# Attention scores as four 64x64-tiled float32 products, in a fused windowed-attention and feed-forward kernel

## The chip, the cores and the metric

The kernel runs on one core of a Trainium2 chip. The metric is the device time of one execution in microseconds; lower is better. Of the kernel before, three timed runs gave 1008.7 us in the median (1007.8 to 1010.62). The engines of the core are named as in the profile: PE (matmuls; PEld is the same engine loading weights), DVE (vector operations), ACT (activations and casts), POOL, and SP, which issues the DMAs.

## What is computed

Attention over a window of 64 positions for 8 batches of 8 heads, 576 positions, head size 64, all float32; then a feed-forward layer with softplus, 512 to 2048 to 512, for all 4608 tokens.

```python
scores = (1 / np.sqrt(64)) * np.matmul(q, k.transpose(0, 1, 3, 2))
rel = pos[:, None] - pos[None, :]
scores = np.where((rel >= 0) & (rel < 64), scores, -1e9)
attn = np.exp(scores - scores.max(-1, keepdims=True))
attn = attn / (attn.sum(-1, keepdims=True) + 1e-9)
x = np.matmul(attn, v)                      # then to 4608 x 512
h = x @ w_in                                # 512 x 2048
g = np.maximum(h, 0.0) + np.log1p(np.exp(-np.abs(h)))
out = g @ w_out                             # 2048 x 512
```

## The kernel before

The 4608 tokens are cut into 12 blocks of 384 (`TB`), a block into three pieces j of 128 queries (`NJ`). Two heads make a pair `hp`; four pairs make the 512 columns of x. A **task** is one block and one pair: 48 tasks. `attention(g, hp)` is a generator; each `yield` ends a stage. The first two blocks (`by_pe`, 8 tasks) run while the weights are still being loaded and converted, and turn the probabilities on PE (L303) and multiply them with v in float32 (L352). The other 40 tasks split q, k, v and the probabilities into high and low parts, use faster matmuls, and turn the probabilities by DMA.

Because a query sees itself and the 63 positions before it, 128 queries need 192 keys. In the 40 later tasks q is cast and its low part subtracted (L241 on ACT, L242 on DVE), then k (L247, L248). For each j four matmuls of 192 columns (two heads, high and low k) go to one PSUM bank (L267). DVE adds the mask, scales and takes the minimum for each head (L274: an instruction and one that reads its accumulator). Since 192 columns hold 128 for each query half, a fold then lays the outer 64 columns over the first (L280). ACT takes exponentials and sums (L284), DVE normalises (L295). The eight early tasks keep k in `kbd`, two heads on a block diagonal with zeros, and do one float32 product of 384 columns for each j (L263).

`ps_a` has three PSUM banks, taken in turn. Up matmuls (`ffn_up`, L390: 12 of 384 columns into `ps_h`) and down matmuls (`ffn_down`, L411: 9 of 512 columns) are the feed-forward layer: 192 steps, each with one up and one down. ACT takes three functions of the up result (L394 to L396), DVE one (L398), ACT or DVE casts (L400) and DVE subtracts (L401).

What sets the order: each stage, each up and each down has a due time, in halves of a step (up of step n at 2n + 0.5, down at 2n + 5.5). All events are sorted by it. `STG` lists the due times of the stages of a task relative to its base; the bases of later tasks are 8 apart (`SHP`), so a task's attention-times-v (L364, one stage for each head) falls where the scores of the task two further on begin. PE keeps this order as it is written; the instructions of the other engines are ordered by a scheduler at build time. [...]

Of the kernel before, what the change touches and what calls it, by code (L numbers as in the profile page):

```python
# [9 lines left out]
F32 = mybir.dt.float32  # L10
# [7 lines left out]
P = 128  # L18
# [13 lines left out]
STG = (-13, -5.9, -5, 0, 1, 2, 3, 4, 5, 6, 7, 7.1, 12, 14, 16, 17)  # L32
# [11 lines left out]
def window_attention_softplus_ffn(  # L44
# [70 lines left out]
    W = CH + P  # L115

    kbd_s = [att.tile([P, 2, CH + TB], F32, name="kbd", tag=f"k{i}") for i in range(2)]
    for t in kbd_s:  # L120
        nc.vector.memset(t[D:P, 0, :], 0.0)
        nc.vector.memset(t[0:D, 1, :], 0.0)
        nc.vector.memset(t[0:D, 0, 0:CH], 0.0)
        nc.vector.memset(t[D:P, 1, 0:CH], 0.0)

    v3z = cpool.tile([P, 2, NJ, 2, 2, D], BF16, name="v3z")
    v_ts = [att.tile([P, 2, NJ, P], F32, name="v_t", tag=n) for n in ("nat", "tr")]
    for t in v_ts:
        nc.vector.memset(t[0:CH, 0, 0, :], 0.0)
# [4 lines left out]
    mask = cpool.tile([P, W], BF16, name="mask")  # L134
    nc.gpsimd.memset(mask, 0.0)
    nc.gpsimd.affine_select(
        out=mask, in_=mask, pattern=[[1, W]], compare_op=ALU.is_gt, fill=FAR, base=0, channel_multiplier=-1
    )
    nc.gpsimd.affine_select(
        out=mask, in_=mask, pattern=[[-1, W]], compare_op=ALU.is_ge, fill=FAR, base=CH, channel_multiplier=1  # L140
    )

    mask_c = cpool.tile([P, W], BF16, name="mask_c")
    nc.gpsimd.tensor_copy(mask_c, mask)
    nc.gpsimd.memset(mask_c[:, 0:CH], FAR)
    ident = att.tile([P, P], F32, name="ident", tag="xf")
# [9 lines left out]
    def load_w(f):  # L156


        if f < NE + 4:
            k = FIRST[f % 4] if f < NE else (4, 6)[f % 2]  # L160
            parts = [(spare(k, [P, 2, DM], w_words.dtype, "raws"), spare(k + 1, [P, 2, DM], F32, "ws"), 0, 2)]
        else:
            parts = [
                (
                    ff.tile([P, 1, DM], w_words.dtype, name="raw"),
                    att.tile([P, 1, DM], F32, name="wh", tag=("v_in", "v12")[m]),
                    m, m + 1,
                )
                for m in range(2)
            ]  # L170
# [18 lines left out]
    def attention(g, hp):  # L189
# [12 lines left out]
        heads = [slice(0, D), slice(D, P)]  # L202

        if by_pe:
            qf = ld.tile([P, 2, TB], F32, name="q_in") if hp % 2 else ld.tile([P, 2, W - P + TB], F32, name="k_in")
            qf = qf[:, 0, 0:TB]
            kf = kbd_s[hp % 2]
            skip = CH if t0 == 0 else 0
            nc.sync.dma_start(qf, qT[c0 : c0 + P, t0 : t0 + TB])
            for hh in range(2):  # L210
                nc.sync.dma_start(kf[heads[hh], hh, skip:], kT[c0 + hh * D : c0 + (hh + 1) * D, t0 - CH + skip : t0 + TB])
        else:
            q_in = ld.tile([P, 2, TB], F32, name="q_in")
            k_in = ld.tile([P, 2, W - P + TB], F32, name="k_in")
            ts, ks = slice(t0, t0 + TB), slice(t0 - CH, t0 + TB)
            for half in heads:
                nc.sync.dma_start(
                    q_in[half, :, :], qT[c0 : c0 + P, ts].rearrange("(h d) t -> d h t", h=2)
                )
                nc.sync.dma_start(  # L220
                    k_in[half, :, :], kT[c0 : c0 + P, ks].rearrange("(h d) t -> d h t", h=2)
                )
        yield

        if by_pe:
# [12 lines left out]
        else:
            q_hl = att.tile([P, 2, TB], F32R, name="q_hl")
            low = heads[1]  # L240
            nc.scalar.copy(q_hl, q_in)  # L241
            nc.vector.tensor_tensor(  # L242
                q_hl[low, :, :], q_in[low, :, :], q_hl[low, :, :].bitcast(F32), ALU.subtract
            )
            yield
            k_hi, k_lo = [att.tile([P, 2, W - P + TB], F32R, name=f"k{i}") for i in range(2)]
            nc.scalar.copy(k_hi, k_in)  # L247
            nc.vector.tensor_tensor(k_lo, k_in, k_hi.bitcast(F32), ALU.subtract)  # L248
        yield

        if g == 0:

            st = spare(FIRST[hp], [P, 2, NJ, W], F32, "st0")
        else:
            st = att.tile([P, 2, NJ, W], F32, name="st", bufs=2)
        mn = att.tile([P, 2, NJ], F32, name="mn", bufs=2)
        sm = att.tile([P, 2 * NJ], F32, name="sm", bufs=2)
        for j in range(NJ):
            sp = bank()
            spv = sp[:, : 2 * W].rearrange("p (h c) -> p h c", h=2)  # L260
            js, kc = slice(j * P, (j + 1) * P), slice(j * P, j * P + W)
            if by_pe:
                mm(spv, qf[:, js], kf[:, :, kc], start=True, stop=True)  # L263
            else:
                for hh in range(2):
                    for i, part in enumerate((k_hi, k_lo)):
                        mm(  # L267
                            spv[:, hh, :], q_hl[:, hh, js], part[:, hh, kc],
                            start=(hh == 0 and i == 0), stop=(hh == 1 and i == 1), skip_group_check=True,
                        )  # L270
            t = ORDER[g] * NJ + j
            m = mask_c if (t * P) % S == 0 else mask_b if (t * P) % S + P > S else mask
            for hh in range(2):
                nc.vector.tensor_tensor_reduce(  # L274
                    st[:, hh, j, :], spv[:, hh, :], m, QSCALE, 3.0e38, ALU.add, ALU.min, mn[:, hh, j : j + 1]
                )
            yield

        sv = st.rearrange("p h j c -> p (h j) c")
        nc.vector.tensor_tensor(sv[:, :, 0:CH], sv[:, :, 0:CH], sv[:, :, P:], ALU.min)  # L280
        for hh in range(2):
            for j in range(NJ):
                i = hh * NJ + j
                nc.scalar.activation(  # L284
                    sv[:, i, 0:P], sv[:, i, 0:P], AF.Exp, bias=mn[:, hh, j : j + 1], scale=-1.0, accum_out=sm[:, i : i + 1]
                )
# [7 lines left out]
        pn = sv[:, :, 0:P]  # L294
        nc.vector.tensor_tensor(pn, pn, sm.unsqueeze(2).to_broadcast([P, 2 * NJ, P]), ALU.mult)  # L295
        if by_pe:

            yield
            pt = att.tile([P, 2, TB], F32, name="pt", tag="q_hl")
            for hh in range(2):  # L300
                pp = bank()
                for j in range(NJ):
                    tp(pp[:, j * P : (j + 1) * P], sv[:, hh * NJ + j, 0:P], ident)  # L303
                nc.scalar.copy(pt[:, hh, :], pp[:, :TB])
        else:
# [8 lines left out]
            nc.scalar.copy(nat[:, 0, :, :], pn)  # L314
            turn(0)
            yield
            nc.vector.tensor_tensor(nat[:, 1, :, :], pn, nat[:, 0, :, :], ALU.subtract)
            turn(1)
            yield
            v_in = att.tile([P, 2, NJ, P], F32, name="v_in")  # L320

            before, own = [v[t : t + TB, c0 : c0 + P].rearrange("(j p) n -> p j n", p=P) for t in (t0 - CH, t0)]
            nc.sync.dma_start(v_in[:, 0, :, :], before)
            nc.sync.dma_start(v_in[0:CH, 1, :, :], own[CH:P, :, :])
            nc.sync.dma_start(v_in[CH:P, 1, :, :], own[0:CH, :, :])
            yield

            v12 = att.tile([P, 2, NJ, 2, 2, D], BF16, name="v12")
            vv = v_in.rearrange("p u j (h d) -> p (u j h) d", h=2)
            v1, v2, v3 = [t.rearrange("p u j h i d -> p (u j h) i d")[:, :, i, :] for t, i in ((v12, 0), (v12, 1), (v3z, 0))]  # L330
# [15 lines left out]
        else:  # L346
            xf = att.tile([P, TB], F32, name="xf")
        for hh in range(2):
            if by_pe:
                for a in range(2 * NJ):  # L350
                    cs = slice(a * CH, (a + 1) * CH)
                    mm(  # L352
                        av[heads[hh], cs], v_t[:, a % 2, a // 2, heads[hh]], pt[:, hh, cs],
                        start=(a == 0), stop=(a == 2 * NJ - 1), skip_group_check=True,
                    )
                if hh == 1:
                    nc.scalar.copy(x_t[0], av[:, :TB])
# [154 lines left out]
```

## Time and profile before

| | |
|---|---|
| median of the three runs | 1008.7 us |
| the profiled execution, and its span | 1013.1 us, 1011.3 us |
| DMA queue of the kernel | 137152 packets, 99.65 MB, 36.8% of 16 engines' span |
| HBM | 73.66 MB read, 10.22 MB written |

The span is the time from the first to the last instruction; 1.8 us lie around it. In the table of groups each row gives the line, engine, operation, output and inputs, shape and count, then the busy time, the mean duration of one in ns, and the idle time just before them with what ended it. Rows of a timeline begin with a start and a length in us, from the span's start, and merge like instructions that follow each other (`x12`). Matmuls are pipelined: a record lasts longer than the distance to the next one's start, so prices of PE are read from starts. Rows of windows give for each stretch its length, then the busy time and count of PE, PEld, DVE, ACT and POOL, the granted PE clock, the DMA share and GB/s.

### The profile page before, as it was taken

Reading aid. Unit: us, or ns where it says so; the run is one execution under the profiler, and the core shown is the slowest. Engines: PE = TensorE matmul, PEld = TensorE weight load, DVE = VectorE, ACT = ScalarE, POOL = GpSimd, SP = SyncE. Lnnn points to the kernel's source line nnn. Section 1 sums busy time; section 2 is a strip of 40 time slices with the busy share of each in tenths; the row PEclk is TensorE's granted clock in tenths of the full one; section 3 lists DMA queues with packets and bytes.
Section 4 is the critical chain, followed back from the end, with each engine's and each line's share of the span. In section 5 each row is a group of like instructions: output and inputs, shape, how many; then the busy total and the mean of one; then the engine's idle time right before and its main releaser. Section 6 shows DMA issues by size and latency. Waiting matters only on the chain.

```text
span 1011.3 us, 17290 instructions
## 1 busy us (share of the span) xinstructions
PE 959.9 (95%) x6240; PEld 851.7 (84%) x6240; DVE 730.4 (72%) x1689; ACT 710.4 (70%) x1673; POOL 3.7 (0%) x14
## 2 busy tenths in 40 slices
PE   6546999999999999999999999999999999999998
PEld 3335888898988998899899998899889989998997
DVE  6897588787777777787777777777768867864332
ACT  4566678787777777777777677777767767865443
POOL 1000000000000000000000000000000000000000
PEclk9767999999999999999999999999999999999999
DMA  5845234443333434333334344433423423410000
GB/s 171 292 164 174 90 125 115 128 116 102 92 99 82 110 86 98 101 91 103 97 83 113 99 82 99 112 74 91 129 70 90 134 66 82 112 32 17 32 1 32
DMA packets 137238, 100.76 MB, mean 100 GB/s; under 512 B 70080, under 2 KB 129216, under 8 KB 135616
## 3 DMA queue, kind: packets, MB, share of 16 engines
q1 hardware_dynamic: 137152, 99.65, 36.8%
q8 instruction: 49, 0.80, 0.3%
q14 instruction: 37, 0.30, 0.1%
HBM read 73.66 MB, written 10.22 MB: 83 GB/s over the span
## 4 chain that ended last, share of the span: by engine, by line
PE 85%; DMA 6%; DVE 4%; ACT 4%; issue 1%; SPq 0%; ACTq 0%; DVEq 0%
PE ps_h L390 37%; PE ps_o L411 36%; PE ps_a L267 5%; PE ps_a L364 4%; DMA raws<-in_w_words_dram 3%; DMA raw<-in_w_words_dram 2%; ACT st L284 1%; DVE ws L178 1%; PE ps_a L263 1%; ACT ws L176 1%; PE ps_a L352 1%; DVE w L183 0%; DVE st L295 0%; DMA k_in<-in_kT_dram 0%; DVE ws L179 0%
## 5 line engine op out<-in xcount | busy, mean ns | idle before, releaser
L390 PE MATMUL ps_h<-x,w 128*128 128x384 f32 x2304 | 440.0, 339 | 0.6 <-ACT x L373 0.4
L411 PE MATMUL ps_o<-w,g 128*128 128x512 f32 x1728 | 433.9, 395 | 4.3 <-DVE g L401 3.1
L390 PEld LDWEIGHTS ps_h<-x,w 128*128 128x128 f32 x2304 | 404.7, 189 | 11.9 <-DVE u L398 1.0
L411 PEld LDWEIGHTS ps_o<-w,g 128*128 128x128 f32 x1728 | 319.5, 189 | 65.5 <-DVE g L401 5.2
L394 ACT ACTIVATE u<-ps_h 128x384 f32<-128x384 f32 x192 | 94.3, 491 | 198.3 <-PE ps_h L390 191.6
L398 DVE SCALAR_TENSOR_TENSOR u<-ps_h,u 128x384 f32<-128x384 f32 x192 | 106.9, 557 | 112.0 <-ACT u L396 109.3
L401 DVE TENSOR_TENSOR g<-u,g 128x384 fp32r<-128x384 f32 x192 | 106.3, 554 | 27.2 <-ACT g L400 25.9
L284 ACT ACTIVATE st<-st,mn 128x128 f32<-128x128 f32 x288 | 111.4, 388 | 9.4 <-DVE st L280 9.3
L274 DVE CUSTOM_DVE_ANT_0 st<-ps_a,mask 128x192 f32<-128x192 f32 x216 | 68.5, 351 | 50.5 <-PE ps_a L267 49.6
L395 ACT ACTIVATE u<-u 128x384 f32<-128x384 f32 x192 | 100.8, 525 | 4.4
L396 ACT ACTIVATE u<-u 128x384 f32<-128x384 f32 x192 | 100.2, 522 | 4.2
L400 ACT CAST g<-u 128x384 fp32r<-128x384 f32 x112 | 57.3, 512 | 31.9 <-DVE u L398 31.5
L267 PE MATMUL ps_a<-k,q_hl 128*128 128x192 f32 x480 | 76.6, 282 | 0.0
L267 PEld LDWEIGHTS ps_a<-k,q_hl 128*128 128x128 f32 x480 | 66.5, 191 | 3.2
L364 PEld LDWEIGHTS <-v 128*128 128x128 bf16 x960 | 44.1, 98 | 17.3 <-issue 17.3
L284 ACT ACTIVATION_READ_ACCUMULATOR st<-st,mn 128x1 f32 x288 | 53.8, 187 | 0.0
L364 PE MATMUL ps_a<-tr,v 128*128 128x64 f16 x960 | 53.6, 194 | 0.0
L364 PE MATMUL ps_a<-tr,v3z 128*128 128x64 f16 x480 | 50.4, 193 | 0.0
L295 DVE TENSOR_TENSOR st<-st,sm 128x768 f32<-128x768 f32 x48 | 45.9, 957 | 1.5
L371 DVE SCALAR_TENSOR_TENSOR xf<-ps_a,xf 64x384 f32<-64x384 f32 x80 | 43.8, 547 | 3.3 <-ACT xf L370 2.0
L248 DVE TENSOR_TENSOR k<-k_in,k 128x896 fp32r<-128x896 f32 x40 | 43.4, 1084 | 0.0
L364 PEld LDWEIGHTS <-v3z 128*128 128x128 bf16 x480 | 42.8, 98 | 0.0
(77 smaller groups left out, 762.2 us busy)
## 6 DMA issues: line engine op xcount, KB each, us to landing
k_in<-in_kT_dram SPq DMA_DIRECT2D x80, 224.0 KB, 3.6
q_in<-in_qT_dram SPq DMA_DIRECT2D x84, 192.0 KB, 3.9
raws<-in_w_words_dram SPq DMA_DIRECT2D x12, 1024.0 KB, 6.2
v_in<-in_v_dram SPq DMA_DIRECT2D x40, 192.0 KB, 2.6
v_in<-in_v_dram SPq DMA_DIRECT2D x80, 96.0 KB, 2.6
out_dram<-raw SPq DMA_DIRECT2D x12, 512.0 KB, 2.8
raw<-in_w_words_dram SPq DMA_DIRECT2D x8, 512.0 KB, 3.7
out_dram<-raw SPq DMA_DIRECT2D x12, 256.0 KB, 3.0
```

The lines of the kernel that those rows point to most:

```text
L267: mm(spv[:, hh, :], q_hl[:, hh, js], part[:, hh, kc], start=(hh == 0 and i == 0), stop=(hh == 1 and i == 1), skip_group_check=True,)
L274: nc.vector.tensor_tensor_reduce(st[:, hh, j, :], spv[:, hh, :], m, QSCALE, 3.0e38, ALU.add, ALU.min, mn[:, hh, j : j + 1])
L284: nc.scalar.activation(sv[:, i, 0:P], sv[:, i, 0:P], AF.Exp, bias=mn[:, hh, j : j + 1], scale=-1.0, accum_out=sm[:, i : i + 1])
L364: mm(av[:, j * P + u * CH : j * P + (u + 1) * CH], w[:, u, j, hh, :, :], tr[:, s, hh * NJ + j, u * CH : (u + 1) * CH], start=(n == 0), sto ...
L390: mm(hv, weight(0, a, f)[:, c * P : (c + 1) * P], x[b][c], start=(i_mm == 0), stop=(i_mm == 3 * NC - 1))
L394: nc.scalar.activation(u, hv, AF.Abs)
L395: nc.scalar.activation(u, u, AF.Exp, scale=-1.0)
L396: nc.scalar.activation(u, u, AF.Ln, bias=1.0)
L398: nc.vector.scalar_tensor_tensor(gf, hv, 0.0, u, ALU.max, ALU.add)
L400: (nc.scalar.copy if g < 2 or f % 2 else nc.vector.tensor_copy)(gt[0], gf)
L401: nc.vector.tensor_tensor(gt[1], gf, gt[0].bitcast(F32), ALU.subtract)
L411: mm(ops[g][j], gt[a][:, js], weight(1, b, f), start=(first and i == 0), stop=(last and i == 2),)
```

## The change

All blocks compute their scores in float32 without a split. For each half u of 128 queries there are 64 queries and exactly 128 keys. A product has 64 rows to contract (one head), 64 queries and 128 keys; with two heads (rows) and two query halves (columns) four products use the four 64x64 tiles of the array. Each head has one bank for all three j. The split of q and k and the fold go; the mask is 128 wide; q, k and v of all blocks are loaded in one way, with two buffers each and earlier for v; the scores of a later task are one stage instead of three; the early tasks' products with v alternate between the heads. `kbd` and the double layouts of v go, and the tiles for weights converted late share other buffers.

```diff
-STG = (-13, -5.9, -5, 0, 1, 2, 3, 4, 5, 6, 7, 7.1, 12, 14, 16, 17)
+STG = (-13, -5, 0, 3, 4, 5, 6, 7, 12, 14, 16, 17)
...
-            q_hl = att.tile([P, 2, TB], F32R, name="q_hl")
-            low = heads[1]
-            nc.scalar.copy(q_hl, q_in)
-            nc.vector.tensor_tensor(
-                q_hl[low, :, :], q_in[low, :, :], q_hl[low, :, :].bitcast(F32), ALU.subtract
-            )
-            yield
-            k_hi, k_lo = [att.tile([P, 2, W - P + TB], F32R, name=f"k{i}") for i in range(2)]
-            nc.scalar.copy(k_hi, k_in)
-            nc.vector.tensor_tensor(k_lo, k_in, k_hi.bitcast(F32), ALU.subtract)
...
+        q_in = ld.tile([P, TB], F32, name="q_in", bufs=2)
+        k_in = ld.tile([P, CH + TB], F32, name="k_in", bufs=2)
...
+        nc.sync.dma_start(q_in, qT[c0 : c0 + P, t0 : t0 + TB])
+        nc.sync.dma_start(k_in[:, skip:], kT[c0 : c0 + P, t0 - CH + skip : t0 + TB])
+        yield
+        v_in = att.tile([P, 2 * NJ, P], F32, name="v_in", bufs=2)
...
+        sps = [bank() for _ in heads]
         for j in range(NJ):
-            sp = bank()
-            spv = sp[:, : 2 * W].rearrange("p (h c) -> p h c", h=2)
-            js, kc = slice(j * P, (j + 1) * P), slice(j * P, j * P + W)
-            if by_pe:
-                mm(spv, qf[:, js], kf[:, :, kc], start=True, stop=True)
-            else:
+            js = slice(j * P, (j + 1) * P)
+            for u in range(2):
+                a = 2 * j + u
                 for hh in range(2):
-                    for i, part in enumerate((k_hi, k_lo)):
-                        mm(
-                            spv[:, hh, :], q_hl[:, hh, js], part[:, hh, kc],
-                            start=(hh == 0 and i == 0), stop=(hh == 1 and i == 1), skip_group_check=True,
-                        )
+                    mm(
+                        sps[hh][halves[u], js], q_in[heads[hh], a * CH : (a + 1) * CH],
+                        k_in[heads[hh], a * CH : (a + 2) * CH], start=True, stop=True,
+                    )
...
                 nc.vector.tensor_tensor_reduce(
-                    st[:, hh, j, :], spv[:, hh, :], m, QSCALE, 3.0e38, ALU.add, ALU.min, mn[:, hh, j : j + 1]
-                )
-            yield
+                    st[:, hh, j, :], sps[hh][:, js], m, QSCALE, 3.0e38, ALU.add, ALU.min, mn[:, hh, j : j + 1]
+                )
+            if by_pe or j == NJ - 1:
+                yield
...
-        nc.vector.tensor_tensor(sv[:, :, 0:CH], sv[:, :, 0:CH], sv[:, :, P:], ALU.min)
```

How the built program moves. On PE, in a later task: the rows before, from the first score block of a task (the others stand behind an up and a down), with what each waits for; `k` and `q_hl` are the split parts, `ps_h` and `x` belong to the up step behind.

```order
L267 MATMUL ps_a<-k_2832,q_hl 128x192 [waits PE_49]
L267 MATMUL ps_a<-k_2833,q_hl 128x192
L267 MATMUL ps_a<-k_2832,q_hl 128x192
L267 MATMUL ps_a<-k_2833,q_hl 128x192
L390 MATMUL ps_h<-x_0_1_1602,w_784 128x384 [waits DVE_49]
```

The same place on PE now. L222 are the score products (two heads in turn), L335 is the up step that was L390.

```order
L222 MATMUL ps_a<-k_in,q_in 64x128 [waits DMAHW2_49,PE_49]
L222 MATMUL ps_a<-k_in,q_in 64x128 [waits PE_49]
L222 MATMUL ps_a<-k_in,q_in 64x128 x2
L222 MATMUL ps_a<-k_in,q_in 64x128 [waits DVE_49] x2
L222 MATMUL ps_a<-k_in,q_in 64x128 x2
L222 MATMUL ps_a<-k_in,q_in 64x128 [waits DVE_49] x2
L222 MATMUL ps_a<-k_in,q_in 64x128 x2
L335 MATMUL ps_h<-x_0_1_1616,w_840 128x384
```

All 12 products now stand in one run, and the first two of the second and third group of four each wait for DVE: for the accumulator read (`mn`) of the same head's reduction of the group before.

On DVE at that place before: L401 ends the step ahead, L274 are the reductions, L371 adds the two parts of another task's attention result, L332 splits v.

```order
L401 TENSOR_TENSOR g_2916<-u,g_2915 128x384 [waits PE_49,Activation_49]
L274 ISA st,mn<-ps_a,mask 128x192 [waits PE_49]
L274 ISA mn 128x1
L274 ISA st,mn<-ps_a,mask 128x192
L274 ISA mn 128x1
L371 SCALAR_TENSOR_TENSOR xf<-ps_a,xf 64x384 [waits Activation_49]
L274 ISA st,mn<-ps_a,mask_b 128x192 [waits PE_49]
L274 ISA mn 128x1
L274 ISA st,mn<-ps_a,mask_b 128x192
L274 ISA mn 128x1
L332 TENSOR_TENSOR v_in<-v_in,v_3084 128x768 [waits DMAHW1_49,DMAHW7_49,DMAHW0_49,Activation_49]
```

And now (L346 was L401, L229 was L274, L316 was L371):

```order
L346 TENSOR_TENSOR g_3075<-u,g_3074 128x384 [waits PE_49,Activation_49]
L229 ISA st,mn<-ps_a,mask 128x128 [waits PE_49]
L229 ISA mn 128x1
L229 ISA st,mn<-ps_a,mask 128x128 [waits PE_49]
L229 ISA mn 128x1
L316 SCALAR_TENSOR_TENSOR xf<-ps_a,xf 64x384 [waits Activation_49]
L229 ISA st,mn<-ps_a,mask_105 128x128 [waits PE_49]
L229 ISA mn 128x1
L229 ISA st,mn<-ps_a,mask_105 128x128 [waits PE_49]
L229 ISA mn 128x1
L229 ISA st,mn<-ps_a,mask 128x128 [waits PE_49]
L229 ISA mn 128x1
```

The six reductions of a task stand closer together, each with its own wait for PE; L346 still stands ahead of the first and L316 between the first pair and the second.

More of the change, by code (lines that the diff above doesn't have):

```diff
@@ L112, in weight @@
         return w_last[m, i, k][:, f % 4, :]
[L115 to L129, printed above, removed]
+    v3z = cpool.tile([P, 2 * NJ, 2, 2, D], BF16, name="v3z")
+    heads = [slice(0, D), slice(D, P)]
+    halves = [slice(0, CH), slice(CH, P)]
     FAR = BIG / QSCALE
-    mask = cpool.tile([P, W], BF16, name="mask")
+    mask = cpool.tile([P, P], BF16, name="mask")
     nc.gpsimd.memset(mask, 0.0)
-    nc.gpsimd.affine_select(
-        out=mask, in_=mask, pattern=[[1, W]], compare_op=ALU.is_gt, fill=FAR, base=0, channel_multiplier=-1
-    )
-    nc.gpsimd.affine_select(
-        out=mask, in_=mask, pattern=[[-1, W]], compare_op=ALU.is_ge, fill=FAR, base=CH, channel_multiplier=1
-    )
[L143 to L146, printed above, removed]
+    for i, half in enumerate(halves):
+        nc.gpsimd.affine_select(
+            out=mask[half, :], in_=mask[half, :], pattern=[[1, P]], compare_op=ALU.is_gt, fill=FAR,
+            base=0, channel_multiplier=-1,
+        )
+        nc.gpsimd.affine_select(
+            out=mask[half, :], in_=mask[half, :], pattern=[[-1, P]], compare_op=ALU.is_ge, fill=FAR,
+            base=CH, channel_multiplier=1,
+        )
+    mask_at = [cpool.tile([P, P], BF16, name=f"mask{i}") for i in range(2)]
+    for half, m in zip(halves, mask_at):
+        nc.gpsimd.tensor_copy(m, mask)
+        nc.gpsimd.memset(m[half, 0:CH], FAR)
+    ident = cpool.tile([P, P], F32, name="ident")
     make_identity(nc, ident)
-    mask_b = cpool.tile([P, W], BF16, name="mask_b")
-    nc.gpsimd.tensor_copy(mask_b, mask)
-    nc.gpsimd.memset(mask_b[CH:P, 0:P], FAR)
     nc.gpsimd.memset(v3z, 0.0)
@@ L347, in attention @@
             xf = att.tile([P, TB], F32, name="xf")
-        for hh in range(2):
[L349 to L357, printed above, removed]
-                    nc.vector.tensor_tensor(x_t[1], av[:, :TB], x_t[0].bitcast(F32), ALU.subtract)
-                yield
-                continue
+        if by_pe:
+            for a, hh in itertools.product(range(2 * NJ), range(2)):
+                cs = slice(a * CH, (a + 1) * CH)
+                mm(
+                    av[heads[hh], cs], v_in[:, a, heads[hh]], pt[:, hh, cs],
+                    start=(a == 0), stop=(a == 2 * NJ - 1), skip_group_check=True,
+                )
+            nc.scalar.copy(x_t[0], av[:, :TB])
+            nc.vector.tensor_tensor(x_t[1], av[:, :TB], x_t[0].bitcast(F32), ALU.subtract)
+            yield
+            return
+        for hh in range(2):
             av = bank()
```

80 lines of the change are left out of this document (25 added, 55 removed).

## The prediction

> **What bounds the kernel now.** I read the busy table of the page first, then the chain that ended last, then the windows by stage, and last the timeline of one attention task.
>
> ```profile
> PE 959.9 (95%) x6240; PEld 851.7 (84%) x6240; DVE 730.4 (72%) x1689; ACT 710.4 (70%) x1673; POOL 3.7 (0%) x14
> PE 85%; DMA 6%; DVE 4%; ACT 4%; issue 1%; SPq 0%; ACTq 0%; DVEq 0%
> 75.00:100.00 25.00, 16.62 (x77) 12.54 (x78) 19.12 (x41) 16.29 (x46) 0.00 (x0) 0.73 0.57 176
> 200.00:400.00 200.00, 199.46 (x1364) 178.88 (x1363) 154.27 (x356) 154.42 (x369) 0.00 (x0) 1.00 0.39 97
> ```
>
> TensorE (PE) carries 85% of the last chain. The windows give PE, weight loads, DVE and ACT, then the granted clock: from 200 to 400 us PE is busy 199.46 of 200 us at clock 1.00, while DVE and ACT have some 45 us to spare. The start is different: from 75 to 100 us PE works 16.62 of 25 us. So in the long middle whatever PE does more or waits for is added to the end, and work taken off DVE and ACT gains nothing there.
>
> One task of a later block, TensorE alone:
>
> ```profile
> 304.11 2.27 PE L390 MATMUL ps_h<-x,w 128*128 128x384 f32 x12
> 306.21 2.25 PE L411 MATMUL ps_o<-w,g 128*128 128x512 f32 x9
> ...
> 308.84 0.67 PE L267 MATMUL ps_a<-k,q_hl 128*128 128x192 f32 x4
> 309.34 2.29 PE L390 MATMUL ps_h<-x,w 128*128 128x384 f32 x12
> ...
> 312.01 0.67 PE L267 MATMUL ps_a<-k,q_hl 128*128 128x192 f32 x4
> 312.53 2.26 PE L411 MATMUL ps_o<-w,g 128*128 128x512 f32 x9
> 314.62 0.59 PE L267 MATMUL ps_a<-k,q_hl 128*128 128x192 f32 x4
> 315.04 2.29 PE L390 MATMUL ps_h<-x,w 128*128 128x384 f32 x12
> ```
>
> From start to next start, the three score blocks of a task take 0.50, 0.52 and 0.42 us: **1.44 us** of PE. They stand apart, with feed-forward matmuls between, and nothing waits.
>
> **The change, part by part.** The scores of a task become one burst of 24 float32 products: for each of three 128-query blocks j, four products on the four 64x64 tiles, head 0 into one PSUM bank and head 1 into another. All three j share these two banks. In the new order of PE above, the second and third group of four wait for DVE, and what they wait for is DVE's mask-and-minimum (L229, before L274) of the group ahead, in the same bank. Behind the waiting matmuls on PE stand the up matmuls, with nothing to fill the gap. Before, each j had a bank of its own.
>
> First the tiles. A float32 product leaves two records in the trace: the eight early tasks issue 12 L352 products each, 96 in all, and L352 has 144 + 48 = 192 records.
>
> ```profile
> L352 PE MATMUL ps_a<-pt,v_t x144: 222/314/369, 14.9 to 107.6; 128*64 128x64 f32 x144
> L352 PE MATMUL ps_o<-pt,v_t x48: 222/222/271, 21.4 to 42.8; 128*64 128x64 f32 x48
> 19.77 0.82 PE L303 MATMUL ps_o<-ident,st 128*128 128x128 f32 x6
> L303 PE MATMUL ps_o<-ident,st 128*128 128x128 f32 x12 | 1.6, 273 | 0.0
> 21.42 1.43 PE L352 MATMUL ps_o<-pt,v_t 128*64 128x64 f32 x24 [0.83 <-ACT pt L304]
> 103.72 0.91 PE L352 MATMUL ps_a<-pt,v_t 128*64 128x64 f32 x12
> 104.56 2.38 PE L390 MATMUL ps_h<-x,w 128*128 128x384 f32 x12
> 106.87 0.91 PE L352 MATMUL ps_a<-pt,v_t 128*64 128x64 f32 x12
> 107.71 2.38 PE L390 MATMUL ps_h<-x,w 128*128 128x384 f32 x12
> ```
>
> A record of 128 float32 columns follows the last after (0.82 - 0.27) / 5 = 0.11 us. One of 64 columns takes (0.91 - 0.22) / 11 = 0.06. Products on different column tiles run side by side: one head's 12 records last 0.91 us, both heads' 24 only 1.43, so the second head adds 0.52 where 12 x 0.06 = 0.72 were due; three records lie over the first head's. Row tiles side by side are in no row. Bounds for the four products of a j: all side by side 2 x 0.11 = 0.22 us; one after another 8 x 0.11 = 0.88. I take the first, as the nearest row shows independent tiles.
>
> Switching to the tiled array and back has a price: from 104.56 to 107.71 are 3.15 us, for an up step (306.21 - 304.11 = 2.10) and 12 records (0.74): 0.31 us more. From 103.72 to 104.56 it is 0.10 over 0.74, the rest lies on the up step. I put 0.1 us ahead of a burst and 0.2 behind it. [...]
>
> Now the waits. DVE around the same burst, and the widths from which its new price comes:
>
> ```profile
> 309.19 0.56 DVE L401 TENSOR_TENSOR g<-u,g 128x384 fp32r<-128x384 f32 x1 [0.58 <-ACT g L400]
> 309.66 0.35 DVE L274 CUSTOM_DVE_ANT_0 st<-ps_a,mask 128x192 f32<-128x192 f32 x1
> 309.94 0.08 DVE L274 DVE_READ_ACCUMULATOR2_ANT mn<- 128x1 f32 x1
> 309.94 0.35 DVE L274 CUSTOM_DVE_ANT_0 st<-ps_a,mask 128x192 f32<-128x192 f32 x1
> 310.22 0.08 DVE L274 DVE_READ_ACCUMULATOR2_ANT mn<- 128x1 f32 x1
> 310.22 0.54 DVE L371 SCALAR_TENSOR_TENSOR xf<-ps_a,xf 64x384 f32<-64x384 f32 x1
> 312.73 0.36 DVE L274 CUSTOM_DVE_ANT_0 st<-ps_a,mask_b 128x192 f32<-128x192 f32 x1 [1.96 <-PE ps_a L267]
> L398 DVE SCALAR_TENSOR_TENSOR u<-ps_h,u 128x384 f32<-128x384 f32 x192 | 106.9, 557 | 112.0 <-ACT u L396 109.3
> L430 DVE COPY raw<-ps_o 128x512 f32<-128x512 f32 x24 | 16.5, 686 | 12.1 <-PE ps_o L411 12.1
> 25.54 0.91 PE L263 MATMUL ps_o<-kbd,q_in 128*128 128x384 f32 x2 [1.20 <-DVE x L358]
> ```
>
> L401 keeps DVE until 309.66, and it waits for ACT, not for DVE's load, so less DVE work doesn't make it earlier. A result of PE reaches DVE 0.05 us after its last record's end (312.01 + 0.67 = 312.68, DVE at 312.73). DVE to PE, I take 0.05 as well (an estimate, from the other direction). A reduction follows the last after 0.28 us at 192 columns. At 128 it is at least 0.19 (in proportion) and at most 0.28; I take 0.22, since 128 columns from 384 to 512 cost 0.686 - 0.557 = 0.13 and so 64 fewer save 0.06. Its minimum is read 0.08 later, and that is what PE waits for.
>
> Set t = 0 at 308.84, where the first score block starts now:
> - j = 0: in by 0.1; the last of eight records starts at about 0.30 (one of 0.11 ahead of it, and 0.09 for three staggered starts), lasts 0.27 and is seen at 0.62. DVE comes at 0.82 (309.66), so this work is hidden. Head 0's minimum: 0.82 + 0.22 + 0.08 + 0.05 = 1.17 at PE; head 1's 0.22 later, 1.39.
> - j = 1: head 1's products follow 1.39: weights 0.05, stagger 0.03, first record 0.11, so the last starts at 1.58 and is seen at 1.90, head 0's at 1.87. Between stands L316 (before L371) on DVE, from 1.26 to 1.80: covered. Minima at PE: 1.87 + 0.35 = 2.22 and 2.44.
> - j = 2: the last record starts at 2.44 + 0.19 = 2.63, streams 0.11; with 0.2 to leave the tiles, the up step stands at **2.94**.
>
> A burst costs 2.94 where 1.44 stood: **+1.50 us**. The trace repeats its pattern for each of 40 tasks (480 records of L267, 12 a task), and the new DVE order in front of a burst is the same for nearly all:
>
> ```profile
> L267 PE MATMUL ps_a<-k,q_hl 128*128 128x192 f32 x480 | 76.6, 282 | 0.0
> L248 DVE TENSOR_TENSOR k<-k_in,k 128x896 fp32r<-128x896 f32 x40 | 43.4, 1084 | 0.0
> L242 DVE TENSOR_TENSOR q_hl<-q_in,q_hl 64x768 fp32r<-64x768 f32 x40 | 38.2, 955 | 1.4 <-ACT q_hl L241 0.2
> L247 ACT CAST k<-k_in 128x896 fp32r<-128x896 f32 x40 | 37.5, 938 | 1.9 <-DMA k_in<-in_kT_dram 1.9
> L241 ACT CAST q_hl<-q_in 128x768 fp32r<-128x768 f32 x40 | 33.3, 832 | 0.0
> L280 DVE TENSOR_TENSOR st<-st 128x384 f32<-128x384 f32 x48 | 26.5, 553 | 0.1
> ```
>
> So 40 x 1.50 = **+60 us**. The splits and the fold that go (43.4 + 38.2 + 26.5 us of DVE, 37.5 + 33.3 of ACT) lie beside PE and count as nothing; PE hides them now, and if DVE bound the burst's wait by its load, each would help, but L401's wait for ACT says it doesn't. The joined, earlier loads of q, k and v cost nothing: their first reader stands 13 and 17 places of half a step behind, tens of us against landings of about 4.
>
> In the first 100 us the same edits remove DVE work (eight folds, 8 x 0.55 = 4.4 us; 48 narrower reductions, 48 x 0.06 = 2.9; the zero fills of kbd, some 2) but the new waits make DVE and PE take turns there too, and conversions of weights (L178 and L179, 1.2 us each) stand between two reductions for which PE waits. Bounds -10 and +10 us; I take 0, as these 9 us are about what eight tasks with two turns of half a us each give back.
>
> The profiled execution took 1013.1 us, 1.8 more than its span: 1013.1 + 60 = 1073. The median of the runs lies 4.4 lower: 1008.7 + 60 = 1068.7, so **1069**. With reductions at 0.19 and the start 10 shorter, two turns of 0.06 less make 1.38 and 1009 + 55 - 10 = 1054; with reductions at 0.28 and the start 10 longer, 1009 + 65 + 10 = 1084.
>
> **Rivals.** (a) The change doesn't do what it says: tiles run less than four wide. If two run at once, eight records take 0.44; j = 0 stays about covered, j = 1 and 2 add 0.2 each: 1.9 a task, 1085. If they run in turn, 0.88: reductions of j = 0 start at 0.97 and 1.19, of j = 1 at about 2.24 and 2.46, j = 2 ends at 3.5 and the up step stands at 3.7: 2.3 a task, 1101. For: the two records of a product need the same tile, so strict order would let only neighbours overlap. Against: three records overlapped in L352. [...]
>
> (b) The clock gate. At the start the clock fell to 0.50 after PE had been idle:
>
> ```profile
> 26.60:29.30 2.70, 0.00 (x0) 0.00 (x0) 2.70 (x10) 1.67 (x7) 0.00 (x0) 0.85 0.79 309
> 29.30:33.00 3.70, 1.51 (x6) 1.14 (x6) 1.85 (x4) 2.58 (x10) 0.00 (x0) 0.50 1.02 407
> ```
>
> In a burst PE streams about 0.8 of 2.9 us. Should each burst cost some 3.4 us at half clock behind it (an estimate from the 3.7 us window), 1.7 us are lost each time: 40 x 1.7 = 68 more, 1137. Against: no gap between streams in a burst is longer than 0.8 us (0.41 to 1.17).
>
> (c) The other side. PE passes over a waiting matmul and runs the up step meanwhile, as it started L352's second head before the first was through. Then only the streams count: 48 records four wide, 48 x 0.11 / 4 = 1.32 against 1.44, -0.12 a task, -5 us: 1004. It decides once waits and switching cost less than 0.12 us a task. Against: PE stood idle 1.20 us at 25.54 for DVE, and a wait at the head of a queue with independent work behind it was nowhere filled.
>
> The waits could go if two engines might use different columns of one bank. [...] Without them a task would cost 1.32 + 0.31 - 1.44 = +0.19 us, 1016.
>
> **How the numbers follow.** Forecast, four wide with DVE's turns: 0.60, 1054 to 1084. Rival (a) 0.26, 1085 to 1101, the start moving it by up to 10. Rival (b) 0.08. Rival (c) 0.04; something between, near 1009, 0.02. The range 1045 to 1111 takes in the forecast and (a). Faster by over 0.3% (about what a measurement can tell) is (c): 0.04; within it 0.02; slower 0.94.
>
> **What would show it.** L222's groups of four in the timeline about 1.1 us apart, each with idle time ended by DVE L229; about 2.9 us from the first L222 to the next L335; windows of 200 us with PE below 190 busy at clock 1.00; the span up by as much as 40 bursts. Wrong it is if no idle time stands before L222, if eight records of a group need 0.44 or 0.88 us, if the clock in the middle falls, or if the first dense feed-forward step comes much earlier or later than now.

## The result, and the profile after

The changed kernel takes 1070.0 us in the median of four runs (1069.6 to 1076.0); the kernel before, timed in the same set, 1008.9 (1007.8 to 1010.6). The ratio is **1.0625** (95% interval 1.0599 to 1.065): slower by 61 us. The profiled execution took 1076.0 us, 62.9 more than that of before.

First the busy table, the shares of the last chain and four windows of the changed kernel, in the order in which those of before were read (each window: start and end, length, then PE, PEld, DVE, ACT, POOL, granted clock, DMA share, GB/s).

```profile
PE 982.1 (91%) x6864; PEld 845.1 (79%) x6864; DVE 629.1 (59%) x1551; ACT 673.6 (63%) x1593; POOL 5.3 (0%) x24
PE 74%; DVE 10%; ACT 8%; DMA 6%; issue 1%; POOL 0%; SPq 0%; ACTq 0%; POOLq 0%; DVEq 0%
75.00:100.00 25.00, 16.66 (x111) 13.54 (x107) 16.91 (x36) 14.01 (x34) 0.00 (x0) 0.80 0.30 96
200.00:400.00 200.00, 190.64 (x1364) 164.11 (x1364) 116.17 (x291) 128.24 (x305) 0.00 (x0) 0.98 0.29 73
400.00:600.00 200.00, 189.81 (x1385) 163.90 (x1384) 119.92 (x307) 131.12 (x314) 0.00 (x0) 1.00 0.25 68
600.00:800.00 200.00, 190.84 (x1374) 165.34 (x1373) 119.53 (x297) 131.30 (x308) 0.00 (x0) 1.00 0.26 70
```

DVE lost 101 us of work (730.4 to 629.1) and ACT 37, and the time rose. In the middle PE is now idle for some 10 of 200 us, where it was idle for 0.5, and PE's share of the chain fell from 85 to 74% while DVE's rose from 4 to 10%.

The burst of one later task, on PE from the timeline (start, length, line, operation, count, idle time before it):

```profile
617.17 0.19 PE L309 MATMUL ps_a<-tr,v3z 128*128 128x64 f16 x1
617.29 0.45 PE L222 MATMUL ps_a<-k_in,q_in 64*64 64x128 f32 x8
618.36 0.65 PE L222 MATMUL ps_a<-k_in,q_in 64*64 64x128 f32 x8 [0.62 <-DVE mn L229]
619.40 0.66 PE L222 MATMUL ps_a<-k_in,q_in 64*64 64x128 f32 x8 [0.40 <-DVE mn L229]
619.99 0.80 PE L335 MATMUL ps_h<-x,w 128*128 128x384 f32 x3
```

and on DVE:

```profile
617.53 0.56 DVE L346 TENSOR_TENSOR g<-u,g 128x384 fp32r<-128x384 f32 x1 [0.58 <-ACT g L345]
618.01 0.28 DVE L229 CUSTOM_DVE_ANT_0 st<-ps_a,mask 128x128 f32<-128x128 f32 x1
618.22 0.08 DVE L229 DVE_READ_ACCUMULATOR2_ANT mn<- 128x1 f32 x1
618.22 0.28 DVE L229 CUSTOM_DVE_ANT_0 st<-ps_a,mask 128x128 f32<-128x128 f32 x1
618.43 0.08 DVE L229 DVE_READ_ACCUMULATOR2_ANT mn<- 128x1 f32 x1
618.43 0.54 DVE L316 SCALAR_TENSOR_TENSOR xf<-ps_a,xf 64x384 f32<-64x384 f32 x1
619.05 0.29 DVE L229 CUSTOM_DVE_ANT_0 st<-ps_a,mask 128x128 f32<-128x128 f32 x1
```

The three groups of four products start at 617.29, 618.36 and 619.40, and the two gaps end with DVE's accumulator read. The first group's records end at 617.74, but DVE reads them only at 618.01, when L346 is through, and L346 had waited 0.58 us for ACT. From 617.29 to 619.99 the scores take 2.70 us of PE. The table of PE's waits shows 97 such waits, about two in each of the 48 tasks (line waited at, then releaser; us in all, times, longest):

```profile
PE ps_a L222 <- DVE mn L229: 69.1, 93, 4.2
PE ps_o L222 <- DVE mn L229: 4.2, 4, 2.2
```

### The profile page after: what moved, and what is told of

The parts are those of the page before. It is cut to its first block, busy times and chain, and to the rows that moved or that the text cites. A ratio compares the mean times of both kernels' runs of the same rounds, so it can differ in the third digit from the quotient of the medians.

```text
span 1074.2 us, 17928 instructions
## 1 busy us (share of the span) xinstructions
PE 982.1 (91%) x6864; PEld 845.1 (79%) x6864; DVE 629.1 (59%) x1551; ACT 673.6 (63%) x1593; POOL 5.3 (0%) x24
## 4 chain that ended last, share of the span: by engine, by line
PE 74%; DVE 10%; ACT 8%; DMA 6%; issue 1%; POOL 0%; SPq 0%; ACTq 0%; POOLq 0%; DVEq 0%
PE ps_h L335 37%; PE ps_o L356 29%; PE ps_a L222 5%; DMA raws<-in_w_words_dram 3%; PE ps_a L309 2%; DVE st L229 2%; DVE g L346 2%; DVE u L343 2%; ACT u L340 2%; ACT u L341 2%; ACT u L339 2%; DMA raw<-in_w_words_dram 1%; ACT g L345 1%; ACT ws L165 1%; DVE ws L167 1%
## 5 line engine op out<-in xcount | busy, mean ns | idle before, releaser
L335 PE MATMUL ps_h<-x,w 128*128 128x384 f32 x2304 | 447.6, 343 | 0.0
L356 PE MATMUL ps_o<-w,g 128*128 128x512 f32 x1728 | 439.1, 398 | 0.4 <-DVE g L346 0.4
L335 PEld LDWEIGHTS ps_h<-x,w 128*128 128x128 f32 x2304 | 412.7, 191 | 20.3 <-issue 7.2
L343 DVE SCALAR_TENSOR_TENSOR u<-ps_h,u 128x384 f32<-128x384 f32 x192 | 107.0, 558 | 205.0 <-ACT u L341 203.6
L222 PE MATMUL ps_a<-k_in,q_in 64*64 64x128 f32 x1104 | 85.5, 311 | 73.0 <-DVE mn L229 69.1
L346 DVE TENSOR_TENSOR g<-u,g 128x384 fp32r<-128x384 f32 x192 | 106.9, 557 | 55.2 <-ACT g L345 50.5
L222 PEld LDWEIGHTS ps_a<-k_in,q_in 64*64 64x64 f32 x1104 | 47.2, 138 | 103.2 <-DVE mn L229 93.2
L229 DVE CUSTOM_DVE_ANT_0 st<-ps_a,mask 128x128 f32<-128x128 f32 x276 | 69.2, 287 | 33.3 <-PE ps_a L222 25.2
L278 DVE TENSOR_TENSOR v_in<-v_in,v 128x768 f32<-128x768 f32 x40 | 38.4, 959 | 46.4 <-ACT v L277 46.4
L309 PEld LDWEIGHTS <-v 128*128 128x128 bf16 x960 | 44.1, 98 | 17.3 <-issue 17.3
L309 PE MATMUL ps_a<-tr,v 128*128 128x64 f16 x960 | 53.6, 194 | 0.0
L268 ACT CAST nat<-st 128x768 f16<-128x768 f32 x40 | 33.3, 833 | 31.7 <-DMA tr<-nat 29.5
L309 PE MATMUL ps_a<-tr,v3z 128*128 128x64 f16 x480 | 50.4, 193 | 0.0
L316 DVE SCALAR_TENSOR_TENSOR xf<-ps_a,xf 64x384 f32<-64x384 f32 x80 | 43.9, 549 | 8.1 <-ACT xf L315 6.9
L271 DVE TENSOR_TENSOR nat<-st,nat 128x768 f16<-128x768 f32 x40 | 38.3, 958 | 15.7 <-ACT nat L268 14.1
```

Source lines behind the costliest of these rows:

```text
L222: mm(sps[hh][halves[u], js], q_in[heads[hh], a * CH : (a + 1) * CH], k_in[heads[hh], a * CH : (a + 2) * CH], start=True, stop=True,)
L229: nc.vector.tensor_tensor_reduce(st[:, hh, j, :], sps[hh][:, js], m, QSCALE, 3.0e38, ALU.add, ALU.min, mn[:, hh, j : j + 1])
L309: mm(av[:, j * P + u * CH : j * P + (u + 1) * CH], w[:, 2 * j + u, hh, :, :], tr[:, s, hh * NJ + j, u * CH : (u + 1) * CH], start=(n == 0) ...
L335: mm(hv, weight(0, a, f)[:, c * P : (c + 1) * P], x[b][c], start=(i_mm == 0), stop=(i_mm == 3 * NC - 1))
L343: nc.vector.scalar_tensor_tensor(gf, hv, 0.0, u, ALU.max, ALU.add)
L346: nc.vector.tensor_tensor(gt[1], gf, gt[0].bitcast(F32), ALU.subtract)
```

## The experiments

In all runs the kernel before was timed beside the others, 1008.3 us in the median in the first set and 1008.1 in the second. The score products stand on L220 or L221 in some of these kernels and on L268 in the old one with one bank, as the lines moved. To compare stages, the table has from each profiled execution the first score record of the first, ninth and last later task, and the mean step of a task, which is (last - ninth) / 31. Each row but its median is a single execution. That of before, 1013.1 us, is at the slow end of its kernel's runs (1006.0 to 1013.1 in the first set), so a few us in the column "first" are not an effect by themselves.

| | first, us | ninth, us | last, us | step, us | median of the runs, us |
|---|---|---|---|---|---|
| before | 141.6 | 289.5 | 888.8 | 19.33 | 1008.9 |
| after | 137.2 | 304.7 | 950.7 | 20.84 | 1070.0 |
| products first | 125.1 | 272.8 | 860.3 | 18.95 | 982.9 |
| three stages | 134.5 | 281.6 | 888.3 | 19.57 | 1012.5 |
| old products, one bank | 137.0 | 313.7 | 1010.6 | 22.48 | 1133.5 |
| products first in later tasks only | 135.0 | 282.0 | 869.6 | 18.95 | 991.1 |
| old products in later tasks only | 133.1 | 280.9 | 880.5 | 19.34 | 1004.6 |
| head by head | 123.7 | 269.2 | 865.0 | 19.22 | 987.6 |
| half by half | 127.0 | 275.6 | 871.7 | 19.23 | 996.3 |
| tile by tile | 124.6 | 273.4 | 886.2 | 19.77 | 1009.7 |

### All products of a task ahead of all its reductions

The same 12 products and six reductions in the same two banks; only the order in which they are written differs, so no product stands behind a reduction of its bank.

```diff
+        for j, u, hh in itertools.product(range(NJ), range(2), range(2)):
+            js, a = slice(j * P, (j + 1) * P), 2 * j + u
+            mm(sps[hh][halves[u], js], q_in[...], k_in[...], start=True, stop=True)
         for j in range(NJ):
             js = slice(j * P, (j + 1) * P)
-            for u in range(2):
-                ...
-                    mm(sps[hh][halves[u], js], q_in[...], k_in[...], start=True, stop=True)
             t = (t0 + j * P) % S
```

> All 24 products of a task first, then its six reductions; nothing else is changed, so PE has no wait inside a burst. Theory (the two turns with DVE in each burst cost the time, the tiles run four wide): a burst lasts 0.10 + 0.05 + 11 x 0.107 + 0.21 = 1.54 us instead of 2.80, so 40 x 1.25 = 50 us go: about 1020 us, and down to 1013 if the early tasks' turns between weight conversions go too. Rival (tiles less than four wide, or DVE's and ACT's order as such): a burst still takes 2.5 us or more, 1055 us or more. Rival (the clock): it would stay below 1.00 after the start.

Measured: 982.9 us (981.3 to 983.8), ratio **0.9731** (0.9695 to 0.9767) against before. Its PE timeline:

```profile
613.88 0.89 PE L220 MATMUL ps_a<-k_in,q_in 64*64 64x128 f32 x24
614.70 2.39 PE L335 MATMUL ps_h<-x,w 128*128 128x384 f32 x12
```

the group of its products (busy time and mean ns of one; then all the idle time in front of it, and what ended that)

```profile
L220 PE MATMUL ps_a<-k_in,q_in 64*64 64x128 f32 x1104 | 44.8, 297 | 3.9 <-POOL v_in L203 3.9
```

and its middle window:

```profile
200.00:400.00 200.00, 200.00 (x1523) 176.99 (x1522) 129.56 (x328) 143.51 (x347) 0.00 (x0) 1.00 0.31 78
```

The products' waits for DVE are gone (one for POOL is left, at the start), and a burst takes 0.82 us from its first start to the up step, where it took 2.70 with them and 1.44 as three blocks before. PE fills the window again. So the waits for DVE are the whole loss and more: without them the tiled products are 25 us faster than the kernel before, and with them 61 us slower. That is 37 us less than the 1020 expected, for two reasons. The expectation counts 24 products a task as the prediction did; a task has 12 (24 records), and its step is 1.89 us shorter than in the changed kernel where 1.25 were put. And the first later task starts 12 us earlier (125.1 against 137.2), of which the expectation allowed for 7.

### The changed kernel with a stage for each j again

```diff
-STG = (-13, -5, 0, 3, 4, 5, 6, 7, 12, 14, 16, 17)
+STG = (-13, -5, 0, 1, 2, 3, 4, 5, 6, 7, 12, 14, 16, 17)
...
-            if by_pe or j == NJ - 1:
-                yield
+            yield
```

> The later tasks' scores in three stages at due times 0, 1 and 2 as before the change, with an up and a down between; banks and reductions as in the change. Theory: the wait for DVE is covered by the matmuls between; each group costs 0.10 + 0.16 + 0.21 + 0.10 = 0.57 us, 1.70 a task against 1.51 before the change: +8 us, about 1017 us, with the early part as in the change 1010 to 1022. Rival (switching the array's mode is what costs): three switches instead of one, so more than 1070 us.

Measured: 1012.5 us (1011.4 to 1013.4), ratio 1.0035 (1.0017 to 1.0053). PE in the timeline:

```profile
614.29 0.45 PE L222 MATMUL ps_a<-k_in,q_in 64*64 64x128 f32 x8
614.67 2.35 PE L334 MATMUL ps_h<-x,w 128*128 128x384 f32 x12
...
617.49 0.45 PE L222 MATMUL ps_a<-k_in,q_in 64*64 64x128 f32 x8
617.87 2.33 PE L355 MATMUL ps_o<-w,g 128*128 128x512 f32 x9
```

With an up or a down step between two groups (they start 3.20 and 2.65 us apart) DVE has its 2 us, and no group of a later task waits, though the banks are shared as in the changed kernel (16 waits for DVE are left, two for each early task). So it is not the sharing that costs 61 us, but sharing with nothing between. A group takes 0.38 us from its first start to the step behind it, and the array is switched three times a task instead of once: the step of a task is 0.62 us longer than with all products first (19.57 against 18.95).

### The kernel before, its three blocks in one bank and one stage

Nothing of the tiles, loads or split is changed; the old products are only given the wait.

```diff
-STG = (-13, -5.9, -5, 0, 1, 2, 3, 4, 5, 6, 7, 7.1, 12, 14, 16, 17)
+STG = (-13, -5.9, -5, 0, 3, 4, 5, 6, 7, 7.1, 12, 14, 16, 17)
...
+        sp = None
         for j in range(NJ):
-            sp = bank()
+            sp = bank() if by_pe or j == 0 else sp
...
-            yield
+            if by_pe or j == NJ - 1:
+                yield
```

> The kernel before with split q and k and 192-column products, but the later tasks' three score blocks in one stage and in one PSUM bank: only the wait is added, no tiles. Theory: PE waits for both reductions of a block before it may write the next: blocks at 0, about 1.5 and 2.9, end at 3.3 instead of 1.44 us: +1.9 a task, about 1085 us (1065 to 1095). Rival (the tiled float32 products are what costs): no more than 1 per cent over 1009 us.

Measured: 1133.5 us (1131.8 to 1138.3), ratio 1.1236 (1.1192 to 1.1279): slower by 125 us. Two bursts in its PE timeline:

```profile
605.08 0.67 PE L268 MATMUL ps_a<-k,q_hl 128*128 128x192 f32 x4
606.60 0.69 PE L268 MATMUL ps_a<-k,q_hl 128*128 128x192 f32 x4 [0.85 <-DVE mn L275]
608.03 1.17 PE L268 MATMUL ps_a<-k,q_hl 128*128 128x192 f32 x4 [0.74 <-DVE mn L275]
608.99 3.41 PE L392 MATMUL ps_h<-x,w 128*128 128x384 f32 x12
...
630.24 0.67 PE L268 MATMUL ps_a<-k,q_hl 128*128 128x192 f32 x4
...
633.71 2.29 PE L392 MATMUL ps_h<-x,w 128*128 128x384 f32 x12
```

In this trace the granted clock falls to half at 608.05 us and is full again at 611.46, 3.41 us later. Windows cut at these times and whole multiples of 3.41 us from them, two over and behind the first burst and two over the second:

```profile
604.63:608.05 3.42, 1.83 (x28) 1.50 (x27) 2.44 (x11) 1.00 (x2) 0.00 (x0) 1.00 0.00 0
608.05:611.46 3.41, 3.41 (x12) 3.41 (x13) 2.19 (x6) 2.44 (x7) 0.00 (x0) 0.50 0.00 0
628.52:631.94 3.42, 2.57 (x29) 1.97 (x28) 3.17 (x9) 2.34 (x5) 0.00 (x0) 1.00 0.33 126
631.94:635.35 3.41, 2.67 (x18) 2.50 (x19) 2.27 (x11) 1.55 (x2) 0.00 (x0) 1.00 0.28 105
```

At 630.24 the up step stands 3.47 us behind the burst's start, where 1.44 were needed before: 2.03 more, 81 us in 40 tasks, where 76 were expected. So the old products wait as well once they are given one bank and one stage: the order of DVE's turns and PE's products is the cause, with the old products as with the tiled ones. The rest is put down to the clock. At 608.05, within the first burst, it falls to half, and the up step behind lasts 3.41 us instead of 2.29. From the first later task to the step behind the last the trace holds half clock for 26 times 3.41 us (its clock is 0.95 in the window from 200 to 400 us and 0.96 from 400 to 600; in the kernel before there is no half clock from 101 us to the end of the span). If half of each is lost, that is an estimate of 26 x 1.71 = **44 us**, which with the 81 make up the 125. (The mean clock over a whole span is no such measure: two runs of the changed kernel with means of 0.991 and 0.966 take 1069.6 and 1069.7 us.)

### Where in the program the gain without waits lies

In one kernel the products stand first only in the 40 later tasks; the eight early tasks keep the order of the changed kernel.

```diff
+        if not by_pe:
+            for j in range(NJ):
+                products(j)
         for j in range(NJ):
...
+            if by_pe:
+                products(j)
```

> Products first, then reductions, in the 40 later tasks only; the eight early ones as in the changed kernel. By the bursts of products_first (0.94 us with the entry, against 2.80), 40 x 1.86 = 74 us of the change's 1070 go: 996 us. The other 13 us of products_first's gain would then come from the early tasks. If it comes to 983 too, the early tasks' order does not matter; if to 1000 or more, they hide more.

Measured: 991.1 us (990.3 to 993.0), ratio 0.9824 (0.9796 to 0.9852). Of the 87 us between the changed kernel and that with all products first, 79 come from the later tasks and 8 from the early ones. The early waits stand in its table of waits up to 145 us:

```profile
PE ps_a L221 <- DVE mn L236: 22.8, 12, 3.4
PE ps_o L221 <- DVE mn L236: 5.0, 4, 2.2
```

28 us of waits cost 8 us at the end. Part of the gain goes into other waits: those of the float32 products with v (L297, L304) for ACT are 6 us here and 14 with all products first, whose rows are

```profile
PE ps_a L297 <- ACT pt L258: 9.9, 9, 2.2
PE ps_o L297 <- ACT pt L258: 4.5, 3, 3.2
```

against

```profile
PE ps_o L304 <- ACT pt L265: 3.4, 2, 3.0
PE ps_a L304 <- ACT pt L265: 3.0, 5, 1.7
```

The other kernel has the early tasks tiled, products first, and the later tasks as before.

```diff
+        if by_pe:
+            sps = [bank() for _ in heads]
+            for j, u, hh in itertools.product(range(NJ), range(2), range(2)):
+                a = 2 * j + u
+                mm(sps[hh][halves[u], j * P : (j + 1) * P], qf[...], kf[...], start=True, stop=True)
+            for j in range(NJ):
+                ...
-        for j in range(NJ):
+        for j in range(0 if by_pe else NJ):
             sp = bank()
```

> The kernel before with only the eight early tasks changed: 64x64-tiled products first, then reductions of 128 columns, no fold, no block-diagonal k. In the changed kernel the first task of the third block begins its scores at 137.2 us instead of 141.6. If the start's gain is real, 1003 to 1006 us, faster than both kernels; if what the early tasks save is given back to weight conversions and DMA, 1008 to 1011 us.

Measured: 1004.6 us (1002.2 to 1007.3), ratio 0.996 (0.9943 to 0.9976), as expected: the early tasks alone, in this order and without waits for DVE, are worth about 4 us. That is not the order of the early tasks in the changed kernel.

### How far products on different tiles run side by side

Three orders of the 12 products, all ahead of the reductions: all of one head first (two row halves of the array in turn), all of one query half first (two column halves), and tile after tile.

```diff
-        for j, u, hh in itertools.product(range(NJ), range(2), range(2)):
+        for j, u, hh in ((j, u, hh) for hh in range(2) for j in range(NJ) for u in range(2)):
...
+        for j, u, hh in ((j, u, hh) for u in range(2) for j in range(NJ) for hh in range(2)):
...
+        for j, u, hh in ((j, u, hh) for hh in range(2) for u in range(2) for j in range(NJ)):
```

> As products_first (983 us), but the products of head 0 first, then those of head 1, the query halves in turn: neighbours use the two column tiles of one row half. Theory (a product starts as soon as its tile is free, with a short look ahead): two side by side, 12 steps of 0.11 us instead of 6, less some three records at the change of head: +0.5 to 0.65 us a task, 1003 to 1009 us. Rival (PE looks over the whole burst): 983 us. Rival (column tiles in one bank are written in turn): 1030 us or more.

> As products_first, but all products of query half 0 first, then of half 1, the heads in turn: neighbours use the two row tiles of one column half, and write two banks. Theory: as for head by head, 1003 to 1009 us. Rival (row tiles side by side only where the columns differ): 1030 us or more. Rival (PE looks over the whole burst): 983 us.

> As products_first, but the three products of each tile in a row, tile after tile. Theory (short look ahead of some three records, as L352 showed): 24 steps less about 9 at the three changes of tile instead of 6: +1.0 us a task, about 1022 us; with no look ahead 24 steps, +1.9 us, 1060 us. Rival (PE looks over the whole burst): 983 us.

Measured: head by head 987.6 us, ratio 0.9792 (0.9754 to 0.9829); half by half 996.3, 0.9878 (0.9841 to 0.9915), these two of two runs each; tile by tile 1009.7, 1.0014 (0.9996 to 1.0032). A burst of the first and of the last in their PE timelines:

```profile
634.39 1.15 PE L220 MATMUL ps_a<-k_in,q_in 64*64 64x128 f32 x24
635.47 1.84 PE L335 MATMUL ps_h<-x,w 128*128 128x384 f32 x9
```

```profile
629.17 1.69 PE L220 MATMUL ps_a<-k_in,q_in 64*64 64x128 f32 x24
630.79 2.38 PE L335 MATMUL ps_h<-x,w 128*128 128x384 f32 x12
```

From the first start to the up step these are 1.08 and 1.62 us, against 0.82 with four tiles in turn; half by half has 1.08 too. The expectations count 24 records here, as there are, and are still too long: they let products overlap by some three records, and in head by head the second head's first record starts 0.28 us behind the first head's first, whose last starts at 0.60. Tile by tile tells most. The starts of the 24 records of a burst (at 273.43 us), in ns from the first:

```
0 160 269 275 378 435 487 544 550 596 653 710 762 819 825 871 928 985 1037 1094 1146 1203 1312 1421
```

The first tile's three products are the chain 0, 160, 269, 378, 487, 596: six records, 109 ns apart after the first. At 275 a second chain begins with the same distances (435, 544, 653, 762, 871), at 550 a third, at 825 a fourth. The views do not name a record's tile; the chains are read from the distances. The semaphores in the trace agree: the first product of head 1, which has a wait of its own, is the record at 550, and the last of head 0, which releases DVE, is the one at 871. By the chains the second tile's first product starts at 275, ahead of the first tile's third at 487, which the program has in front of it. In strict order, by an estimate from the same distances, each tile would begin 0.49 us after the one ahead, and the burst would last 3 x 0.49 + 0.60 + 0.20 = 2.27 us. It lasts 1.62, and by these starts the products on different tiles did not start strictly in the order of the program.

Head by head and half by half have the same burst and the same step, and yet 8.7 us between them. In the profiled executions 6.4 us are there by the ninth later task (269.2 against 275.6), so they come from the early part: 3.3 from ahead of the first later task (123.7 against 127.0), and most of the rest from one up step behind it, before which PE waits 2.89 us for L343 in half by half and 1.38 in head by head, and which in half by half runs at half clock, 3.91 us instead of 2.35. Why one order of products does better there stays open.

## Why the prediction was right, and where its numbers were not

**The mechanism and its price.** The three turns came at the times given. From where the old blocks started (the last L309 starts at 617.17; 0.03 behind is the old start, 617.20):

| | predicted, us | measured, us |
|---|---|---|
| DVE comes to the first result | 0.82 | 0.81 |
| second group, first head | 1.17 | 1.16 |
| second group, other head | 1.39 | 1.37 |
| third group, first head | 2.22 | 2.20 |
| up step | 2.94 | 2.79 |
| the same, with its first record's longer distance | 2.94 | 2.90 |

The up step starts 0.20 us after the burst's last record where 0.31 (0.11 to stream, 0.2 to leave the tiles) was put; but its own second matmul follows 0.28 us later, where 0.17 are usual, so the rest of the price lies there. The 0.03 us from one staggered start to the next and the 0.05 us for weights in the prediction's sum were the author's estimates and stand in no row: the four products of the first group start 6 to 7 ns apart, and from first to last start its eight records take 0.18 us where 0.20 were put, those of the second group from head 1's first on 0.17 where 0.19 were put. The step of a task rose from 19.33 to 20.84 us, **1.51 where 1.50 was put**. That they agree to 0.01 is luck. From start to next start, in the mean of 30 later tasks, (2.79 - 1.44) = 1.35 are the burst with its entry and 0.05 lie on the four up steps, 0.10 less than put; the last 0.10 lies on the four down steps (8.44 us against 8.35), which the prediction took as unchanged. It is there with all products first (8.44) and in the old kernel with one bank (8.46) too, so it needs neither the tiles nor the waits; what it comes from is open. PE in the windows of 200 us, put below 190, is busy for 190.6, 189.8 and 190.8.

**Removed work worth nothing.** The 101 us of DVE and 37 of ACT that went bought nothing that shows in the middle: DVE comes to the burst when ACT lets L346 go, and with all products first PE is busy for 200.00 of 200 us. No run puts the splits back beside the tiled products, so this rests on the traces.

**The start, taken as 0.** Here two errors cancel. In the profiled executions the first later task starts 4.4 us earlier (137.2 against 141.6). That the change does this is not shown: in the old kernel with one bank, whose early tasks are as before, it starts at 137.0. And in its burst and the next ones the reductions stand between weight conversions (the PE timeline):

```profile
137.17 0.45 PE L222 MATMUL ps_a<-k_in,q_in 64*64 64x128 f32 x8
140.03 0.65 PE L222 MATMUL ps_a<-k_in,q_in 64*64 64x128 f32 x8 [2.41 <-DVE mn L229]
142.78 0.91 PE L222 MATMUL ps_a<-k_in,q_in 64*64 64x128 f32 x8 [2.10 <-DVE mn L229]
```

and DVE in its second wait:

```profile
140.24 0.43 DVE L166 TENSOR_SCALAR wh<-wh 128x512 uint32<-128x512 uint32 x1
140.75 0.69 DVE L172 TENSOR_TENSOR w<-wh,w 128x512 fp32r<-128x512 f32 x1
141.36 0.55 DVE L346 TENSOR_TENSOR g<-u,g 128x384 fp32r<-128x384 f32 x1
141.83 0.69 DVE L167 SCALAR_TENSOR_TENSOR wh<-raw,wh 128x512 uint32<-128x512 uint32 x1
142.43 0.28 DVE L229 CUSTOM_DVE_ANT_0 st<-ps_a,mask 128x128 f32<-128x128 f32 x1
```

This burst lasts 6.4 us. The order of DVE in front of a burst, said to be the same for nearly all, is another one for the first eight steps: by the ninth later task the kernel is 15.2 us behind, so these steps lost (15.2 + 4.4) / 8 = 2.45 us each, 0.95 more than the later ones. They did not lose it evenly: the first step is 4.5 us over the later ones' loss, the three in which the clock falls to half behind a burst (rival (b)) are 1.2, 1.8 and 1.9 over it, and the others at or below it. The first step is long with all products first too (21.64 us against 17.30 before), where PE waits 3.0 us for L343, so the turns are not its only cause. The sum that was measured: -4.4 + 39 steps x 1.51 + 8 x 0.95 + 1.0 from the last burst to the end = 63, against 60. The forecast of 1069 fits the median of 1070.0; its 1073 for the profiled execution stands against 1076.

**Rival (a), less than four wide.** It fell. The eight records of a task's first group start at 0, 7, 13, 20, 160, 167, 173 and 180 ns, four at a time, and with their ends take the 0.45 us of the row at 617.29.

**Rival (b), the clock.** The chance of 0.08 was for a real thing. In the changed kernel the clock falls to half in or behind four bursts of the first later tasks (at 141.24 us for 6.83, at 199.27, 219.75 and 264.12 for 3.41 us each, where the rival put 3.4), for instance (windows of a burst and of what follows):

```profile
217.00:219.70 2.70, 1.31 (x18) 0.69 (x18) 2.12 (x11) 1.99 (x8) 0.00 (x0) 1.00 0.00 0
219.70:223.10 3.40, 3.40 (x16) 3.05 (x17) 1.80 (x9) 1.65 (x8) 0.00 (x0) 0.51 0.41 121
```

and from 400 to 800 us none: clock 1.00. In the old kernel with one bank, with bursts of 3.47 us, it took some 44 us. The argument against it, that no gap between streams is longer than 0.8 us, was the wrong test: there, with the same gaps of 0.85 and 0.74 us, the clock fell to 0.50 in the burst at 605.08 and stayed at 1.00 through the one at 630.24, and what differed between them was how they lay in the stretches of 3.41 us (last section). That the middle of the changed kernel stayed at 1.00 was a near thing (a busy share of 0.70 there, of 0.69 ahead of a fall).

**Rival (c), faster.** In tile by tile PE did pass over waiting products (the second tile's first started at 275 ns, the first tile's third at 487), but those waited for their tile. In the changed kernel's burst the products that waited for DVE held up the step behind them (the idle 0.62 and 0.40 us above). The prices of this rival and of the burst without waits were wrong: the prediction counted 24 products and 48 records a task, where three groups of four make 12 and 24. Without waits a task was put at +0.19 us and the kernel at 1016; measured are -0.38 a task and 982.9. No run leaves the waits out in the order of the changed kernel, so whether they could go there is not shown. The forecast itself counts eight records a group and isn't touched.

## What to carry to other kernels

Where several results share a PSUM bank, write all matmuls into it ahead of the first instruction that reads it, or put other matmuls between: the same instructions in another order were 1070 or 983 us, and 1012.5 with a step between. Before less work on other engines is taken for a gain, look on the engine that bounds for each wait that the new order brings, follow what its releaser stands behind, and price the turn from that. Count products and records from the loops once more when the sum is done.

## What the runs showed of the hardware beyond that

In tile by tile PE started products on one tile ahead of older ones that waited for theirs, by the chains above: the second tile's first at 275 ns, the first tile's third at 487. The burst took 1.62 us, where strict order is estimated at 2.27.

The granted clock fell to half behind stretches in which PE was busy for more than half of the time, in one for 1.83 of 3.42 us. In the traces of the kernel before and of the changed one it holds each of its values for a whole multiple of 3.41 us (once to 267 times) between the first change and the last. In the old kernel with one bank, of the bursts shown, that at 605.08 lies for the most part in one stretch of 3.42 us, with those 1.83 us of PE, and the next stretch is at 0.50. The burst at 630.24 lies across two stretches, with 2.57 and 2.67 busy, and the clock stays at 1.00: these two like bursts differ by where they fall. In the changed kernel, of the stretches at full clock in the time of the later tasks, those with a busy share of 0.19 (137.83 us), 0.60 (195.85), 0.59 (216.33) and 0.69 (260.71) were followed by half clock; the lowest from 267.53 us to the last burst, at 0.70, were not.
